# Turning K and P on VectorE instead of transposing them on TensorE, in a one-token attention layer

## The chip, the cores and the metric

The kernel runs on one core of a Trainium2 chip. The metric is the device time of one execution in microseconds (us); a smaller one is better. The four executions of the kernel before lie within 0.06% of each other (384.63 to 384.87 us). The profiles are of single executions, and the span of a profile is about 2 us shorter than the time. Engines are named as in the profile: PE is TensorE (PEld its weight loads), DVE is VectorE, ACT is ScalarE, POOL is GpSimd, and SP issues the DMA loads.

## The reference, cut to what matters

Four sequences each decode one token. The last 4096 positions of a cached K and V are attended to, with 16 K/V heads of 128 and two query heads for each; then come an output projection and a gated feed-forward layer. Nearly all of the bytes are K and V.

```python
B, Hq, Hkv, Dh, W = 4, 32, 16, 128, 4096
q = (layernorm(x) @ wq)                        # [B, Hq, Dh]
k = repeat(k_cache[:, :, Sk - W:, :], 2)       # bf16, 64 MiB of it are read
v = repeat(v_cache[:, :, Sk - W:, :], 2)       # 64 MiB
p = softmax(q @ k.T * Dh ** -0.5)
h = x + (p @ v) @ wo
out = h + ((relu(n(h) @ W_gate)) * (n(h) @ W_up)) @ W_down
```

## The kernel before

K and V come in 16 tiles of 4 MiB each (K0 to K15 and V0 to V15; a tile is one sequence and four K/V heads), through a ring of four slots in SBUF. A load into a slot waits until the last reader of the slot is done. A K tile has positions on its partitions, but this kernel's Q times K takes the 128 numbers of a head on the partitions, so TensorE transposes it, 128x128 at a time, into PSUM (2048 times, 140.3 us busy), and VectorE and ScalarE copy it out (87.0 and 123.0 us):

```python
def pe_tr(i):                       # 4 a tile; 32 transposes each
    for j in range(4):
        for u in range(8):
            ...
            pe(..., lambda e: e.transpose(out=bankb[TRB[j]][:, u * 128:(u + 1) * 128],
                                          in_=kn[:, t, :], identity=perm...))      # L425
def evac(i, j):
    dst = kT[i // 2 % 2][:, lo:lo + 1024]
    if j % 2 == 0: dve(..., e.tensor_copy(out=dst, in_=src), deps)                 # L439
    else:          act(..., e.copy(out=dst, in_=src), deps)                        # L441

def pe_qk(dd):                      # 2 a tile; 16 matmuls of 32 columns of weights each
    for a in range(4):
        for j in range(4):          # each j to 32 partitions of its own; 16 matmuls took 0.98 us
            pe(..., lambda e: e.matmul(bank[4 + w][32 * j:32 * j + 32, :],         # L457
                lhsT=qTm[:, b, 4 * qd + a, :], rhs=k[:, j, :, a, :], ...))

place((kind, g), off, TILE, ("TR", 4 * g + 3) if kind == "K" else ("PV", 4 * g + 3), ...)
#                           the last reader, which frees the slot
```

P is transposed on TensorE as well (128 times) and copied out under a mask by VectorE. Softmax, P times V, and the layers after attention are cut here.

Of the kernel before, what the change touches and what calls it, by code (L numbers as in the profile page):

```python
# [6 lines left out]
ALU = mybir.AluOpType  # L7
# [4 lines left out]
B = 4  # L12
# [9 lines left out]
NUNIT = 4 * NTILE  # L22
# [5 lines left out]
KTW = 8192  # L28
# [86 lines left out]
def bass_sequential_preLN__sliding_block_cached__glu_gated_reglu__decode_kernel(  # L115
# [12 lines left out]
    with ExitStack() as es:  # L128
# [12 lines left out]
        arena = sb("arena", [128, 2 * KTW + NSLOT * TILE], BF16)  # L141
# [6 lines left out]
        c_m4 = sb("c_m4", [128, 4, 32], FP32)  # L148
        c_qm = sb("c_qm", [128, 4, 32], FP32)
        c_e8 = sb("c_e8", [128, 8, 16], FP32)  # L150
        c_s4 = sb("c_s4", [128, 4, 4], FP32)
        perm = sb("perm", [128, 4, 32], BF16)
        m4 = sb("m4", [128, 4], FP32)
        par = sb("par", [128, 2], FP32)
        am8 = sb("am8", [128, 8], FP32)
# [16 lines left out]
        qTm = sb("qTm", [128, B, KVH, 32], BF16)  # L172
        stat = sb("stat", [128, B, 8], FP32)
        gm4 = sb("gm4", [1, 128], FP32)
        fq = sb("fq", [128, 4], FP32)
# [19 lines left out]

        kT = [arena[:, i * KTW:(i + 1) * KTW] for i in range(2)]
        slot0 = 2 * KTW

# [3 lines left out]
        TRB = (0, 1, 2, 3)  # L202
        s_ps = psb[:, 4:6, :].rearrange("p a b -> p (a b)")
        o_ps = bank[6]
        m_ps = bank[7]
        mb_ps = bankb[7]
# [25 lines left out]
        def add_kv(kind, g):  # L232
            b, qd = divmod(g, 4)
            s = ring_slot()
            off = slot0 + s * TILE
            cache = A_k_cache if kind == "K" else A_v_cache
            src = cache[b, 4 * qd:4 * qd + 4, SK - WIN:SK, :].rearrange("a (p t) d -> p a (t d)", p=32)
            place((kind, g), off, TILE, ("TR", 4 * g + 3) if kind == "K" else ("PV", 4 * g + 3),
                  lambda e: e.dma_start(out=arena[:, off:off + TILE], in_=src), key=f"slot{s}")
# [19 lines left out]
        for blk in range(2 * KTW // 64):  # L259
            owner[blk] = "QKEND"  # L260
# [24 lines left out]
        def kv(kind, i):  # L285
            off = land[(kind, i // 4)]
            return arena[:, off:off + TILE].rearrange("p (t d) -> p t d", d=DH)

# [5 lines left out]
        pool("c_perm0", lambda e: e.memset(perm[:, :, :], 0.0))  # L294
        pool("c_perm", lambda e: e.affine_select(out=perm[:, :, :], in_=perm[:, :, :], pattern=[[-1, 4], [-4, 32]],
                                                 compare_op=ALU.not_equal, fill=1.0, base=0, channel_multiplier=1), ["c_perm0"])
# [6 lines left out]
                                                compare_op=ALU.not_equal, fill=1.0, base=0, channel_multiplier=1), ["c_m40"])  # L303
        pool("c_ones", lambda e: e.memset(ones_f[:, :], 1.0))
# [20 lines left out]
        for j in range(4):  # L325
            pool(f"c_same{j + 1}", lambda e, j=j: e.affine_select(out=sameh[:, :, :], in_=sameh[:, :, :], pattern=[[0, 4], [-1, 32]],
                                                                compare_op=ALU.not_equal, fill=0.25, base=-32 * j,
                                                                channel_multiplier=1), [f"c_same{j}"])

        pool("c_toq0", lambda e: e.memset(toq[:, :, :, :], 0.0))  # L330
        for q in range(4):
# [10 lines left out]
        dve("c_am8", lambda e: e.tensor_copy(out=am8[:, :].rearrange("p (a h) -> p a h", h=2),  # L342
                                             in_=bass.AP(tensor=m4, offset=0, ap=[[4, 128], [1, 4], [0, 2]])), ["c_m4"])
        dve("c_qTm", lambda e: e.memset(qTm[:, :, :, :], 0.0))
# [23 lines left out]
        def pe_q():  # L368
# [4 lines left out]
            for c in range(DC):  # L373
                pe("TP1", lambda e, c=c: e.transpose(out=tpv[:, 32 + c * 4:32 + (c + 1) * 4],
                                                     in_=chunk(x_bf, xd_bf[:, :, :].rearrange("b r a -> b (r a)"), c),
                                                     identity=ident_b[0:B, 0:B]))
            for c in range(DC):
# [7 lines left out]
            for bk in range(2):  # L385
                for s in range(4):
                    blk = bk * 4 + s
                    pe(("QT", blk), lambda e, blk=blk: e.transpose(out=mb_ps[:, blk * 128:(blk + 1) * 128],
                                                                   in_=p_sb[:, blk * 128:(blk + 1) * 128], identity=ident_b[:, :]),
                       [f"qev{bk}"] if s == 0 else [])  # L390

        def dve_q():
# [5 lines left out]
            dve("xT", lambda e: e.tensor_copy(out=xT[:, :, :], in_=tpv[:, 32:52].rearrange("p (c b) -> p c b", b=B)))  # L398
            dve("qev0", lambda e: e.tensor_copy(out=p_sb[:, 0:512], in_=bank[4]), ["QMM"])
            for s in range(8):  # L400
                hh4, bk = s % 4, s // 4
                off = 34 * (bk * 8 + hh4 // 2) + hh4 % 2
                dst = bass.AP(tensor=qTm, offset=off, ap=[[B * KVH * 32, 128], [68, 4], [KVH * 32, B]])
                dve("qTm", lambda e, dst=dst, s=s: e.tensor_copy(  # L404
                    out=dst, in_=mb_ps[:, s * 128:(s + 1) * 128].rearrange("p (g b) -> p g b", b=32)[:, :, 0:4]),
                    [("QT", 7), "c_qTm"])
# [5 lines left out]
        def pe_tr(i):  # L412
            kn = kv("K", i)
            for j in range(4):
                for u in range(8):
                    t = j * 32 + i % 4 * 8 + u
                    deps = []
                    if u == 0:
                        deps = [("L", "K", i // 4)] if j == 0 else []
                        if i == 0:  # L420
                            deps.append("c_perm")
                        else:
                            deps.append(("EV", i - 1, j))
                    last = j == 3 and u == 7
                    o = pe(("TRJ", i, j), lambda e, j=j, u=u, t=t: e.transpose(  # L425
                        out=bankb[TRB[j]][:, u * 128:(u + 1) * 128], in_=kn[:, t, :],
                        identity=perm[:, :, :].rearrange("p a k -> p (a k)")), deps)
                    if last:
                        P.names[("TR", i)] = o

        def evac(i, j):
            lo = j * 2048 + i % 2 * 1024
            dst = kT[i // 2 % 2][:, lo:lo + 1024]
            src = bankb[TRB[j]][:, 0:1024]
            deps = [("TRJ", i, j)]
            if i >= 4:
                deps.append(("QK", i // 2 - 2))
            if j % 2 == 0:
                dve(("EV", i, j), lambda e: e.tensor_copy(out=dst, in_=src), deps)  # L439
            else:  # L440
                act(("EV", i, j), lambda e: e.copy(out=dst, in_=src), deps)  # L441

        def pe_qk(dd):
            g, w = divmod(dd, 2)
            b, qd = divmod(g, 4)
            k = kT[dd % 2].rearrange("p (j t a k) -> p j t a k", j=4, t=16, a=4)
            for a in range(4):
                for j in range(4):
                    deps = []
                    if a == 0:  # L450
                        deps.append(("EV", 2 * dd + 1, j))
                        if qd == 0 and j == 0:
                            if b == 0:
                                deps += ["qTm", "qev0", "qev1"]
                            else:
                                deps += [("EXP", b - 1, w), ("MAX", b - 1)]
                    o = pe(("QK", dd), lambda e, a=a, j=j: e.matmul(  # L457
                        bank[4 + w][32 * j:32 * j + 32, :], lhsT=qTm[:, b, 4 * qd + a, :], rhs=k[:, j, :, a, :],
                        start=(qd == 0 and a == 0), stop=(qd == 3 and a == 3), skip_group_check=True), deps)
            P.names["QKEND"] = o  # L460

        def softmax(b, w):
            if w == 0:
                dve(("MAX", b), lambda e: e.tensor_reduce(out=stat[:, b, 0:1], in_=s_ps, axis=AX.X, op=ALU.max, negate=True),  # L464
                    [("QK", 8 * b + 7)])
                dve(("NB", b), lambda e: e.tensor_scalar(out=stat[:, b, 1:2], in0=stat[:, b, 0:1], scalar1=SCALE, scalar2=None,  # L466
                                                         op0=ALU.mult), [("MAX", b)])
            act(("EXP", b, w), lambda e: e.activation(  # L468
                out=p_sb[:, 2048 * w:2048 * w + 2048].rearrange("p (k a) -> p k a", a=4),
                in_=bass.AP(tensor=psb, offset=(4 + w) * 512, ap=[[4096, 128], [1, 512], [0, 4]]), func=ACT.Exp,  # L470
                bias=stat[:, b, 1:2], scale=SCALE, accum_out=stat[:, b, 2 + 3 * w:3 + 3 * w]),
                [("NB", b), ("PT", b - 1, 3) if b else ("QT", 7)])

        def put_pT(b, r):
            for tl in range(8):
                deps = []
                if tl == 0:
                    deps = [("EXP", b, r // 2)]
# [246 lines left out]
```

## Time and profile before

| | before |
|---|---|
| time, median of 4 runs | 384.68 us |
| input queue's share of 16 engines' time | 97.4% |
| PE, DVE, ACT busy | 65%, 42%, 38% |

From the page of the kernel before: of its slices (40 equal parts of the span, each digit tenths of busy time; PEclk is the granted TensorE clock in tenths), its DMA queues (packets, MB, share of 16 engines) and its chain of waits (share of the span by line).

```profile
PE   0664999779492938893947667966759366026753
...
PEclk9997999999888796999796969996969657555597
DMA  8999999999999999999999999999999999999992
...
q1 hardware_dynamic: 6352, 159.59, 97.4%
...
DMA sb_arena<-in_A_k_cache_dram 53%; PE psb L425 18%; DMA sb_arena<-in_B_W_down_dram 8%; DMA sb_arena<-in_A_v_cache_dram 8%; PE psb L457 5%; PE psb L505 2%; PE psb L480 1%; DVE sb_pp L487 1%; ACT sb_pp L468 1%; SPq L280 0%; DVE sb_stat L464 0%; DVE sb_o_sel L516 0%; PE psb L539 0%; PE psb L530 0%; DVE sb_o_tmp L512 0%
```

DMA stands at 9 from the second slice to the last but one: the kernel is as fast as its loads. The chain passes through PE only where a transpose frees a slot; a load of K took 28.3 us (median) from issue to landing, where the queue, at 429 GB/s from 31 to 281 us, moves a tile in about 9.8 us (an estimate: 4.19 MB at that rate). So a load waits behind others for most of its time, and this wait should cost nothing (the repair v4 below, which has no transposes, takes the same time).

The groups of instructions that the change touches (line, engine, operation, shape, count, then busy us, mean ns of one, and the idle time before with what ended it):

```profile
L425 PE MATMUL psb<-sb_perm,sb_arena 128*128 128x128 bf16 x2048 | 140.3, 235 | 74.0 <-DMA sb_arena<-in_A_k_cache_dram 73.8
L441 ACT COPY sb_arena<-psb 128x1024 bf16<-128x1024 bf16 x128 | 123.0, 1021 | 141.1 <-PE psb L425 141.1
...
L439 DVE COPY sb_arena<-psb 128x1024 bf16<-128x1024 bf16 x128 | 87.0, 689 | 112.1 <-PE psb L425 111.6
...
L457 PE MATMUL psb<-sb_arena,sb_qTm 128*32 128x512 bf16 x512 | 38.0, 423 | 0.9 <-DVE sb_qTm L404 0.9
```

A mean of a matmul is its latency; matmuls overlap: the 512 of L457, at a mean of 423 ns, would add up to 217 us, and their busy time is 38.0 us. What one costs in a stream is the busy time over the count: the four-abreast QK matmuls of L457 cost 38.0 us / 512 = 74 ns each.

The prediction rests on two more lines, weight loads of 128 columns at full clock (granted clock 1.00 from 27.5 to 28.4 and from 370.8 to 371.6 us), from the view of one source line (duration ns min/median/max). L667 reads its weights at a step of 18 bytes, L388 contiguously.

```profile
L667 PEld LDWEIGHTS psb<-sb_ident_b,sb_pp x9: 138/145/159, 370.8 to 371.3; 128*128 128x128 bf16 x9
...
L388 PEld LDWEIGHTS psb<-sb_ident_b,sb_pp x8: 95/98/98, 27.6 to 28.0; 128*128 128x128 bf16 x8
```

### The profile page before, as it was taken

How to read it: one execution, taken by the hardware profiler on the slowest of the kernel's cores; microseconds unless marked ns; L12 is line 12 of the kernel's file. 1: busy time of each engine (PE TensorE's matmuls, PEld its weight loads, DVE VectorE, ACT ScalarE, POOL GpSimd, SP SyncE). 2: the span in 40 equal slices, each digit the busy share in tenths (PEclk: the TensorE clock that was granted, in tenths of full speed). 3: DMA queues.
4: the chain of work that ended last, by engine and by line, in shares of the span. 5: the costliest groups of instructions: out<-in, count | busy, mean ns of one | idle time of the engine just before them, and what ended most of it. 6: DMA issues, size and time to landing. Idle time of an engine off the chain costs nothing.

```text
span 382.6 us, 8170 instructions
## 1 busy us (share of the span) xinstructions
PE 248.7 (65%) x3781; PEld 185.9 (49%) x3781; DVE 159.0 (42%) x277; ACT 146.4 (38%) x162; POOL 8.7 (2%) x36
## 2 busy tenths in 40 slices
PE   0664999779492938893947667966759366026753
PEld 0643788557371726672726455745546222003532
DVE  3342565665342434774432426752516454002220
ACT  3341688836161524762433428542525401000010
POOL 7100000000000000000000000000000000000000
PEclk9997999999888796999796969996969657555597
DMA  8999999999999999999999999999999999999992
GB/s 329 439 433 432 410 421 437 434 433 433 425 423 433 427 433 435 427 420 433 437 430 435 424 428 427 427 428 439 437 432 415 421 436 451 416 431 426 416 411 113
DMA packets 6408, 160.09 MB, mean 418 GB/s; under 512 B 740, under 2 KB 744, under 8 KB 1384
## 3 DMA queue, kind: packets, MB, share of 16 engines
q1 hardware_dynamic: 6352, 159.59, 97.4%
q8 instruction: 29, 0.48, 0.5%
q14 instruction: 3, 0.02, 0.0%
q10 hardware_dynamic: 24, 0.01, 0.0%
HBM read 159.58 MB, written 0.00 MB: 417 GB/s over the span
## 4 chain that ended last, share of the span: by engine, by line
DMA 69%; PE 27%; DVE 2%; SPq 1%; ACT 1%; issue 0%
DMA sb_arena<-in_A_k_cache_dram 53%; PE psb L425 18%; DMA sb_arena<-in_B_W_down_dram 8%; DMA sb_arena<-in_A_v_cache_dram 8%; PE psb L457 5%; PE psb L505 2%; PE psb L480 1%; DVE sb_pp L487 1%; ACT sb_pp L468 1%; SPq L280 0%; DVE sb_stat L464 0%; DVE sb_o_sel L516 0%; PE psb L539 0%; PE psb L530 0%; DVE sb_o_tmp L512 0%
## 5 line engine op out<-in xcount | busy, mean ns | idle before, releaser
L425 PE MATMUL psb<-sb_perm,sb_arena 128*128 128x128 bf16 x2048 | 140.3, 235 | 74.0 <-DMA sb_arena<-in_A_k_cache_dram 73.8
L441 ACT COPY sb_arena<-psb 128x1024 bf16<-128x1024 bf16 x128 | 123.0, 1021 | 141.1 <-PE psb L425 141.1
L425 PEld LDWEIGHTS psb<-sb_perm,sb_arena 128*128 128x128 bf16 x2048 | 131.5, 106 | 89.3 <-DMA sb_arena<-in_A_k_cache_dram 79.8
L439 DVE COPY sb_arena<-psb 128x1024 bf16<-128x1024 bf16 x128 | 87.0, 689 | 112.1 <-PE psb L425 111.6
L505 PE MATMUL psb<-sb_arena,sb_pp 128*32 128x512 bf16 x512 | 35.9, 425 | 19.9 <-DMA sb_arena<-in_A_v_cache_dram 19.9
L457 PE MATMUL psb<-sb_arena,sb_qTm 128*32 128x512 bf16 x512 | 38.0, 423 | 0.9 <-DVE sb_qTm L404 0.9
L505 PEld LDWEIGHTS psb<-sb_arena,sb_pp 128*32 128x32 bf16 x512 | 12.9, 104 | 36.3 <-DMA sb_arena<-in_A_v_cache_dram 20.9
L512 DVE TENSOR_TENSOR sb_o_tmp<-psb,sb_qm 128x512 f32<-128x512 f32 x16 | 11.1, 692 | 41.2 <-PE psb L505 41.2
L487 DVE TENSOR_TENSOR sb_pp<-psb,sb_am 128x1024 bf16<-128x1024 bf16 x16 | 19.6, 1223 | 16.2 <-PE psb L480 16.2
L480 PE MATMUL psb<-sb_ident_b,sb_pp 128*128 128x128 bf16 x128 | 11.5, 242 | 15.8 <-DVE sb_pp L487 8.3
L468 ACT ACTIVATE sb_pp<-psb,sb_stat 128x2048 bf16<-128x2048 f32 x8 | 15.8, 1975 | 9.7 <-DVE sb_stat L466 9.7
L457 PEld LDWEIGHTS psb<-sb_arena,sb_qTm 128*32 128x32 bf16 x512 | 11.6, 103 | 14.8 <-issue 6.2
L480 PEld LDWEIGHTS psb<-sb_ident_b,sb_pp 128*128 128x128 bf16 x128 | 8.6, 108 | 18.8 <-ACT sb_pp L468 8.1
L516 DVE TENSOR_REDUCE sb_o_sel<-sb_o_tmp 128x128 f32<-128x512 f32 x16 | 16.4, 1024 | 0.5
L612 ACT COPY sb_pp<-psb 128x288 f32<-128x288 f32 x1 | 0.4, 399 | 36.2 <-PE psb L607 36.2
L654 PE MATMUL psb<-sb_arena,sb_hnT 128*32 128x384 bf16 x120 | 7.5, 421 | 4.1 <-DVE sb_hnT L639 2.2
L654 PEld LDWEIGHTS psb<-sb_arena,sb_hnT 128*32 128x32 bf16 x120 | 4.1, 121 | 7.2 <-DMA sb_arena<-in_B_W_up_dram 2.3
L464 DVE TENSOR_REDUCE sb_stat<-psb 128x1 f32<-128x1024 f32 x4 | 4.9, 1221 | 4.6 <-PE psb L457 4.6
L687 PE MATMUL psb<-sb_arena,sb_pp 128*32 128x144 bf16 x144 | 3.7, 251 | 4.1 <-DMA sb_arena<-in_B_W_down_dram 3.6
L534 ACT ACTIVATE sb_stat<-sb_stat 128x1 f32<-128x1 f32 x4 | 0.9, 213 | 13.1 <-DVE sb_stat L532 13.1
L661 DVE TENSOR_TENSOR sb_pp<-psb,sb_pp 128x384 bf16<-128x384 f32 x3 | 1.5, 551 | 9.6 <-PE psb L654 9.6
L687 PEld LDWEIGHTS psb<-sb_arena,sb_pp 128*32 128x32 bf16 x144 | 2.6, 105 | 5.1 <-DMA sb_arena<-in_B_W_down_dram 4.6
(128 smaller groups left out, 78.7 us busy)
## 6 DMA issues: line engine op xcount, KB each, us to landing
sb_arena<-in_A_k_cache_dram SPq DMA_DIRECT2D x16, 4096.0 KB, 28.3
sb_arena<-in_A_v_cache_dram SPq DMA_DIRECT2D x16, 4096.0 KB, 33.6
sb_arena<-in_A_wo_dram SPq DMA_DIRECT2D x1, 4608.0 KB, 20.7
sb_arena<-in_B_W_gate_dram SPq DMA_DIRECT2D x1, 4608.0 KB, 34.1
sb_arena<-in_B_W_up_dram SPq DMA_DIRECT2D x1, 4608.0 KB, 43.5
sb_arena<-in_A_wq_dram SPq DMA_DIRECT2D x1, 4096.0 KB, 23.0
sb_arena<-in_B_W_down_dram SPq DMA_DIRECT2D x3, 1296.0 KB, 30.0
sb_arena<-in_B_W_down_dram SPq DMA_DIRECT2D x1, 864.0 KB, 31.6
```

Source lines behind the costliest of these rows:

```text
L425: o = pe(("TRJ", i, j), lambda e, j=j, u=u, t=t: e.transpose(out=bankb[TRB[j]][:, u * 128:(u + 1) * 128], in_=kn[:, t, :], identity=perm[: ...
L439: dve(("EV", i, j), lambda e: e.tensor_copy(out=dst, in_=src), deps)
L441: act(("EV", i, j), lambda e: e.copy(out=dst, in_=src), deps)
L457: o = pe(("QK", dd), lambda e, a=a, j=j: e.matmul(bank[4 + w][32 * j:32 * j + 32, :], lhsT=qTm[:, b, 4 * qd + a, :], rhs=k[:, j, :, a, :], ...
L468: act(("EXP", b, w), lambda e: e.activation(out=p_sb[:, 2048 * w:2048 * w + 2048].rearrange("p (k a) -> p k a", a=4), in_=bass.AP(tensor=p ...
L480: pe(("PT", b, r), lambda e, tl=tl: e.transpose(out=mb_ps[:, tl * 128:(tl + 1) * 128], in_=p_sb[:, (r * 8 + tl) * 128:(r * 8 + tl + 1) * 128],
L487: dve(("PM", b, r), lambda e: e.tensor_tensor(out=dst, in0=src, in1=msk, op=ALU.mult), [("PT", b, r), "c_am8", ("PV", 16 * b - 1) if b els ...
L505: pe(("PV", i), lambda e, j=j, lo=lo, pm=pm, tb=tb: e.matmul(o_ps[32 * j:32 * j + 32, :], lhsT=pT[:, pm:pm + 32], rhs=v[:, lo:lo + 512], s ...
L512: dve(("OS", g), lambda e: e.tensor_tensor(out=o_tmp[:, :].rearrange("p (t d) -> p t d", t=4), in0=o_ps.rearrange("p (t d) -> p t d", t=4) ...
L516: dve(("OSEL", g), lambda e: e.tensor_reduce(out=o_sel[:, qd, :], in_=o_tmp[:, :].rearrange("p (t d) -> p d t", t=4), axis=AX.X, op=ALU.ad ...
L654: pe(("GU", g, c // 4), lambda e, g=g, m=m, j=j, lo=lo, c=c: e.matmul(bank[3 * g + m][32 * j:32 * j + 32, 0:384], lhsT=hnT[:, c if c < 4 e ...
L687: pe("DOWN", lambda e, j=j, r=r, n=n, wv=wv: e.matmul(bank[0][32 * n:32 * n + 32, 0:144], lhsT=hhT[:, r * 128 + 32 * j:r * 128 + 32 * j + 32],
```

## The change

Its intent is to take the transposes and their copies out of PE, PSUM and ACT. The change is written for a transpose on VectorE of 32x32 blocks of 4-byte elements, so that a pair of bf16 numbers moves as one element. K is turned so in place. In the layout meant, a partition then holds one pair index of 32, in each quarter of 32 partitions for other positions; a column holds a row of the tile, and the two numbers of a pair lie side by side. Q times K then needs q in blocks on the diagonal of a full 128x128 weight, one matmul for each head `a` and each of four parts `cb` of the 128 numbers. As the rows of a K tile are ordered position by position with the four heads inside (partition = 4 p + a), the columns of one head are every fourth pair: the moving operand steps by 8 elements, 16 bytes.

```diff
-            place((kind, g), off, TILE, ("TR", 4 * g + 3) if kind == "K" else ("PV", 4 * g + 3),
+            place((kind, g), off, TILE, ("QK", g, 1) if kind == "K" else ("PV", g),
...
-        def pe_tr(i): ...            # 32 transposes, 4 times a tile
-        def evac(i, j): ...          # and their copies out of PSUM
+        def turn_k(g, w):
+            k = arena[:, land[("K", g)] + w * QWW:][:, 0:QWW].bitcast(FP32)
+            dve(("TRA", g, w), lambda e: e.transpose(out=k, in_=k), ...)              # L420
...
         def pe_qk(g, w):
             for a in range(4):
-                for j in range(4):
-                        bank[4 + w][32 * j:32 * j + 32, :], lhsT=qTm[:, b, 4 * qd + a, :], rhs=k[:, j, :, a, :],
+                for cb in range(4):
+                    off = land[("K", g)] + w * QWW + cb // 2 * 64 + 2 * a + cb % 2
+                        bank[SB[b % 2] + w], lhsT=arena[:, wo_:wo_ + 128],            # L437
+                        rhs=bass.AP(tensor=arena, offset=off, ap=[[AW, 128], [128, 64], [8, 8]]),
...
+            for w in range(2):       # softmax: the scores read four times, masked by the bias, each time into another fourth of P
+                for a in range(4):
+                    act(("EXP", b, w), lambda e, w=w, a=a: e.activation(                # L458
+                        out=bass.AP(tensor=pp, offset=4096 + 2048 * w + a, ap=[[8192, 128], [4, 512]]), ...
+        def turn_p(b, w):            # instead of 128 TensorE transposes and masked copies
+            dve(("PTR", b, w), lambda e: e.transpose(out=dst, in_=src), ...)
```

Cut here: the code that lays q into the blocks, a second pair of PSUM banks for the scores, the softmax weights, and renamed waits. The work after attention is the same.

## The prediction

> **What bounds the kernel now.** The DMA queue. The view of DMA queues gives 160.09 MB and 97.4% of the time of all 16 engines for the input queue; the slices show DMA at 9 everywhere but at the ends, at 410 to 450 GB/s. PE is 65%, DVE 42%, ACT 38% busy. The chain of waits names K loads for 53% and the line of TensorE transposes for 18%, but that is how slots are released; about three loads are queued (28.3 us from issue to landing, for tiles of about 9.75 us), so the queue does not run dry.
>
> **What the change removes.** 2048 transposes (140.3 us of PE), their evacuations (ACT 123.0 us, DVE 87.0 us), 128 transposes of P (11.5 us) and their masked copies (19.6 us of DVE). Almost none of it delays the input queue, so the gain is about 0.
>
> **What it adds.**
> 1. 32 in-place turns of 128x4096 fp32 on DVE. [...] The trace's DVE operations of 512 and 1024 elements (692 and 1221 ns) give 1.03 ns per element, so an estimate of 4.4 us each, 8.8 us per K tile, 140 us in all. It fits beside 9.75 us (K alone) and 19.5 us (K and V).
> 2. QK: still 512 matmuls of 512 columns, but of full width, no longer four side by side. Before, 16 took 0.98 us, so four side by side 0.245 us. At that rate a K tile takes 7 to 8 us. But the moving operand now steps by 16 bytes. [...] The trace has a hint: weight loads of 128 columns with a step of 18 bytes took 145 ns, contiguous ones 98 ns, both at full clock. So I expect near 430 ns per matmul: 13.8 us per K tile, 220 us in all, above the 9.75 us at which the first K tiles arrive.
> 3. K0's slot is released only after q exists (about 31 us) and QK of K0 is done, no longer by transposes at 22 us.
>
> **On the critical path.** I played both cases through with these durations, four slots, queues in order. At 216 to 260 ns the queue runs dry once, before K3, for 1.5 to 3 us. At 430 ns: before K3 about 8 us, before V1 2.5 us, before K6 about 12 us (K4, softmax and PV come together), then hardly again, since K and V together give 19.5 us for 16 to 17 us of PE; 20 to 26 us in all. The tail (last weights, last matmuls) stays.
>
> **Prediction.** 402 us; 384.5 to 413 holds it 8 times in 10. Two humps: about 387 if the strided read is free, about 406 if it halves. Faster by over 2%: 0.03; within 2%: 0.40; slower by over 2%: 0.57.
>
> **What would show it.** QK matmuls spaced near 430 ns or near 216; DVE turns at 4.4 us; holes in the DMA slices at about 45 to 50 and 100 to 115 us and hardly any later; PE busy all through the first 120 us; ACT far down.
>
> **What would make it wrong.** Strided reads at full rate (then "same"); turns at twice my cost (then DVE binds too, 410 and more); QK above 450 ns, where PE binds later too and each 40 ns adds some 20 us; slots freed sooner than I think.

The 4.4 us of a turn follow from the 1.03 ns per element of the trace. The 430 ns of a QK matmul, and with them the 20 to 26 us of holes and the case of 406 us, stays as the author's estimate: twice the 216 ns (median) at which groups of four matmuls of the kernel before follow each other at full clock (L457 and L505). That such a read takes twice the time, no trace had shown; the weight loads alone say 145 / 98 = 1.48 times. The forecast came to 402 us, between the cases of 387 and 406.

## The result, and the profile after

The changed kernel takes 625.8 us (median of 4 runs, 624.17 to 626.28) against 384.68 us: the ratio is 1.626 (95% interval 1.6237 to 1.6283), 63% slower. Ratios here and below are the mean time of one kernel's fast runs over that of the other's of the same rounds, so not quite the ratio of the medians. The time lies far outside the predicted range.

The page of the changed kernel, the same parts as before:

```profile
PE   0399999995989999979989999969899999833556
...
PEclk9955555555565656555565656565655555566577
DMA  8971952606066484848092848483482929349996
...
q1 hardware_dynamic: 6352, 159.59, 60.6%
...
PE psb L437 71%; PE psb L480 6%; DMA sb_arena<-in_B_W_down_dram 5%; DMA sb_arena<-in_A_v_cache_dram 4%; DMA sb_arena<-in_A_wq_dram 3%; DVE sb_arena L420 2%; ACT sb_pp L458 2%; DVE sb_o_sel L492 1%; DVE sb_stat L444 1%; PE psb L382 1%; DVE sb_o_tmp L488 1%; PE psb L446 0%; PE psb L452 0%; DVE sb_pp L467 0%; ACT sb_arena L412 0%
```

PE and DMA have changed places. DMA has holes through the whole of the attention, not in the first 120 us alone, and PE is at 9 nearly everywhere, at half clock. 71% of the chain is the QK matmul. Its group and those of the other new work:

```profile
L437 PE MATMUL psb<-sb_arena 128*128 128x512 bf16 x512 | 441.5, 1035 | 6.7 <-DVE sb_arena L420 4.6
L420 DVE STREAM_TRANSPOSE sb_arena<-sb_arena 128x4096 f32<-128x4096 f32 x32 | 141.4, 4431 | 33.4 <-DMA sb_arena<-in_A_k_cache_dram 33.4
...
L458 ACT ACTIVATE sb_pp<-psb,sb_stat 128x512 bf16<-128x512 f32 x32 | 39.4, 1459 | 479.3 <-DVE sb_stat L453 479.3
```

QK costs 441.5 / 512 = 862 ns a matmul, twice what I had put down, and 27.6 us a K tile, where a K and a V tile together arrive in about 19.5 us (an estimate: 8.39 MB at the 429 GB/s of the kernel before). The turns cost 4.43 us each, as estimated. The waits of the DMA queue's own issuer (us in total, times, longest) say what held the loads:

```profile
SPq L240 <- PE psb L437: 482.8, 16, 55.1
```

That sum alone is no loss: in the contiguous kernel below the same wait adds up to 252.6 us while the queue is busy for 97.8%. The holes in the DMA slices are the loss.

Three readings of this trace narrow the cause before any experiment. First, the clock. Half clock could be the cause or the consequence. At the end of each of the first 12 PVs, give or take 0.7 us, the granted clock goes from 0.50 to 1.00 for 3.4 us (one ends at 214.30 us, and the clock is 1.00 from 214.87 to 218.29 us). From the timeline, here are the weight loads of four successive QK matmuls in such a stretch (start us, us):

```profile
215.07 0.12 PEld L437 LDWEIGHTS psb<-sb_arena 128*128 128x128 bf16 x1 [0.72 <-issue]
215.93 0.11 PEld L437 LDWEIGHTS psb<-sb_arena 128*128 128x128 bf16 x1 [0.74 <-issue]
216.78 0.12 PEld L437 LDWEIGHTS psb<-sb_arena 128*128 128x128 bf16 x1 [0.74 <-issue]
217.65 0.11 PEld L437 LDWEIGHTS psb<-sb_arena 128*128 128x128 bf16 x1 [0.74 <-issue]
```

And the view of that stretch (its length; busy us and count of PE, PEld, DVE, ACT, POOL; granted clock; DMA share; GB/s):

```profile
214.90:218.20 3.30, 3.30 (x5) 0.46 (x4) 3.27 (x3) 0.00 (x0) 0.00 (x0) 1.00 1.11 477
```

At a clock of 1.00 the matmuls are still 0.86 us apart. Over the whole trace the 19 gaps that lie in full clock have a median of 857 ns, and so have the 469 in half clock. So the clock is not the cause: the columns follow at 857 / 512 = 1.67 ns each at a clock of 1.00 as at 0.50. That the clock follows the access pattern is shown by a run below: with that pattern alone changed, the mean granted clock of the profiled run is 0.778 instead of 0.573.

Second, the company. VectorE turns K in place while QK runs. From 31.14 us on, QK ran without a pause for over 90 us. VectorE turned three tiles meanwhile, for 8.8 us each, and was idle for up to 61 us in between. Up to 141 us, the 24 spacings of QK that lie inside a turn have a median of 857 ns, the other 103 one of 859. So the turns do not slow it.

Third, the stages. From 31 to 141 us PE was busy for 109.86 of 110 us, all of it QK of the first four K tiles; no load can be called late there. The view of that stretch, with the columns as above:

```profile
31.00:141.00 110.00, 109.86 (x128) 15.76 (x128) 26.31 (x6) 1.30 (x5) 0.00 (x0) 0.50 0.47 196
```

What is left are the step of the moving operand, and the width of the matmul.

### The profile page after: what moved, and what is told of

The parts are those of the page before. It is cut to its first block, busy times and chain, and to the rows that moved or that the text cites. A ratio compares the mean times of both kernels' runs of the same rounds, so it can differ in the third digit from the quotient of the medians.

```text
span 623.9 us, 3670 instructions
## 1 busy us (share of the span) xinstructions
PE 531.7 (85%) x1629; PEld 102.0 (16%) x1629; DVE 209.7 (34%) x158; ACT 51.2 (8%) x94; POOL 16.2 (3%) x38
## 4 chain that ended last, share of the span: by engine, by line
PE 79%; DMA 12%; DVE 6%; ACT 2%; issue 0%; SPq 0%
PE psb L437 71%; PE psb L480 6%; DMA sb_arena<-in_B_W_down_dram 5%; DMA sb_arena<-in_A_v_cache_dram 4%; DMA sb_arena<-in_A_wq_dram 3%; DVE sb_arena L420 2%; ACT sb_pp L458 2%; DVE sb_o_sel L492 1%; DVE sb_stat L444 1%; PE psb L382 1%; DVE sb_o_tmp L488 1%; PE psb L446 0%; PE psb L452 0%; DVE sb_pp L467 0%; ACT sb_arena L412 0%
## 5 line engine op out<-in xcount | busy, mean ns | idle before, releaser
L437 PE MATMUL psb<-sb_arena 128*128 128x512 bf16 x512 | 441.5, 1035 | 6.7 <-DVE sb_arena L420 4.6
L420 DVE STREAM_TRANSPOSE sb_arena<-sb_arena 128x4096 f32<-128x4096 f32 x32 | 141.4, 4431 | 33.4 <-DMA sb_arena<-in_A_k_cache_dram 33.4
L437 PEld LDWEIGHTS psb<-sb_arena 128*128 128x128 bf16 x512 | 61.9, 123 | 368.4 <-issue 361.4
L458 ACT ACTIVATE sb_pp<-psb,sb_stat 128x512 bf16<-128x512 f32 x32 | 39.4, 1459 | 479.3 <-DVE sb_stat L453 479.3
L480 PE MATMUL psb<-sb_arena,sb_pp 128*32 128x512 bf16 x512 | 54.6, 605 | 21.8 <-DMA sb_arena<-in_A_v_cache_dram 14.9
L467 DVE STREAM_TRANSPOSE sb_pp<-sb_pp 128x2048 bf16<-128x2048 bf16 x8 | 18.0, 2281 | 1.9 <-ACT sb_pp L458 1.9
L382 PE MATMUL psb<-sb_arena,sb_xnT 128*32 128x512 bf16 x32 | 3.6, 631 | 8.8 <-DMA sb_arena<-in_A_wq_dram 8.8
L458 ACT ACTIVATION_READ_ACCUMULATOR sb_pp<-psb,sb_stat 128x1 f32 x32 | 10.2, 318 | 0.0
L298 POOL MEMSET sb_arena<- 128x8192 f32 x1 | 6.9, 6924 | 0.0
L412 ACT COPY sb_arena<-sb_q_keep 32x128 bf16<-32x128 bf16 x16 | 4.9, 305 | 2.0 <-DVE sb_q_keep L404 1.9
```

The costliest lines, as they stand in the source:

```text
L298: pool("c_qW", lambda e: e.memset(arena[:, 0:2 * QWW].bitcast(FP32), 0.0))
L382: pe("QMM", lambda e, c=c, w=w, g=g, bk=bk: e.matmul(bank[4 + bk][32 * g:32 * g + 32, :], lhsT=xnT[:, c + bk if c == 4 else c, :], rhs=w, ...
L412: act(("QW", b), lambda e, i=i: e.copy(out=bass.AP(tensor=arena, offset=32 * i * AW + b % 2 * QWW + 32 * i, ap=[[AW, 32], [128, 4], [514, ...
L420: dve(("TRA", g, w), lambda e: e.transpose(out=k, in_=k), [("L", "K", g)] if w == 0 else [])
L437: pe(("QK", g, w), lambda e, off=off, wo_=wo_, qd=qd, first=first, last=a == cb == 3: e.matmul(bank[SB[b % 2] + w], lhsT=arena[:, wo_:wo_ ...
L458: act(("EXP", b, w), lambda e, w=w, a=a: e.activation(out=bass.AP(tensor=pp, offset=4096 + 2048 * w + a, ap=[[8192, 128], [4, 512]]), in_= ...
```

## The experiments

The kernels marked wrong read other elements of K than they should. They keep every instruction, wait and shape of the changed kernel. The comparison with the reference passed them too, since the scores of these inputs are small and the softmax nearly flat; so it does not vouch for an order of K. For the repairs (v1 to v5) I worked the order out element by element on indices against the changed kernel's.

### Four steps of the moving operand in one kernel (wrong)

A line, in this and the later texts, is a stretch of 16 bytes within a partition. That the price goes by lines is a theory, called LINE, for the runs to test.

```diff
-   rhs=bass.AP(tensor=arena, offset=off, ap=[[AW, 128], [128, 64], [8, 8]])
+   batch 0: [[AW, 128], [128, 64], [8, 8]]     batch 1: [[AW, 128], [128, 64], [4, 8]]
+   batch 2: [[AW, 128], [128, 64], [2, 8]]     batch 3: [[AW, 128], [128, 64], [1, 8]]
+   (off without the term 2 * a + cb % 2 + cb // 2 * 64)
```

> The changed kernel with the QK moving operand read at another step in each of the four batches (wrong results on purpose; the same 16 x 32 matmuls, the same widths, weights and waits): 8 runs of 8 elements as now at step 8 (16 bytes) in batch 0, step 4 (8 bytes) in batch 1, step 2 in batch 2, step 1 in batch 3. Theory LINE: each time the next column lies in another 16-byte line the moving operand costs about 1.67 ns (857 ns over 512 columns), at whatever clock; more columns of the same line come free up to the array's rate. Then the four groups are spaced about 857, 430, 216 and 216 ns (430 where the granted clock is 0.5), and the whole is about 455 to 465 us. Rival STEP: any step over 1 costs the full price: 857, 857, 857, 216 and about 560 us. Rival WIDE: it is the full-width 128x128 matmul with new weights each time, or the turns in place running beside it, not the step: 857 in all four and 626 us.

One run, 455.31 us. Each batch has a source line of its own; L441, L443, L445, L447 are batches 0 to 3:

```profile
L441 PE MATMUL psb<-sb_arena 128*128 128x512 bf16 x128 | 110.2, 1037 | 2.1 <-ACT sb_arena L412 2.1
L443 PE MATMUL psb<-sb_arena 128*128 128x512 bf16 x128 | 55.8, 607 | 6.0 <-DVE sb_arena L420 6.0
...
L447 PE MATMUL psb<-sb_arena 128*128 128x512 bf16 x128 | 38.0, 469 | 13.1 <-DVE sb_arena L420 13.1
...
L445 PE MATMUL psb<-sb_arena 128*128 128x512 bf16 x128 | 35.8, 442 | 14.2 <-DVE sb_arena L420 14.1
```

Busy time over 128 gives 861, 436, 280 and 297 ns. The last two mix full and half clock; their gaps in full clock have medians of 217 and 216 ns. So WIDE falls: full-width matmuls with new weights run at 216 ns. STEP falls too: a step of 4 bytes costs nothing (217 against 216 ns), and one of 8 bytes half as much as one of 16 (436 and 861 ns), as the lines that they touch say. LINE stands. (This trace has no clock record before 155.4 us, so the full clock that its page shows for batch 0 is not measured.)

### Patterns that part the line from the step (wrong)

```diff
+   batch 0: [[AW, 128], [128, 64], [7, 8]]           batch 1: [[AW, 128], [128, 64], [16, 8]]
+   batch 2: [[AW, 128], [128, 64], [16, 4], [1, 2]]  batch 3: [[AW, 128], [128, 64], [1, 4], [8, 2]]
```

> As d1_steps, with patterns that part lines from steps (wrong results on purpose). Batch 0: step 7 (14 bytes; 8 columns touch 7 lines): LINE says 7/8 of 857, about 750 ns. Batch 1: step 16 (32 bytes): LINE says 857 as at 16 bytes; if the step itself mattered, about twice that. Batch 2: two adjacent columns, then 32 bytes on: LINE says half, 430 ns, although the average step is 16 bytes; a price on the step of the outer dimension would say 857. Batch 3: the same two lines visited in turn, one column from each (step 8 inside, step 1 outside, so only 2 distinct lines in 8 columns): 857 if what counts is that the next column lies in another line, about 216 if lines just read are kept. Whole about 540 to 565 us under LINE.

One run, 527.86 us. L441 to L447 are again batches 0 to 3:

```profile
L443 PE MATMUL psb<-sb_arena 128*128 128x512 bf16 x128 | 118.1, 1096 | 4.6 <-DVE sb_arena L420 4.6
L441 PE MATMUL psb<-sb_arena 128*128 128x512 bf16 x128 | 109.4, 1036 | 2.1 <-ACT sb_arena L412 2.1
...
L447 PE MATMUL psb<-sb_arena 128*128 128x512 bf16 x128 | 69.2, 699 | 0.0
L445 PE MATMUL psb<-sb_arena 128*128 128x512 bf16 x128 | 56.1, 610 | 1.4 <-DVE sb_arena L420 1.4
```

Two of four came as LINE said. Two neighbours and then a jump of 32 bytes cost 56.1 / 128 = 438 ns, half, although the average step is 16 bytes. A step of 32 bytes costs 923 ns, 7% over 16 bytes and not twice. The others were misses: step 7 cost 855 ns where its 7 lines out of 8 columns should give 750, and two lines visited in turn cost 541 ns, neither 857 nor 216. The whole is also under the 540 to 565 us expected.

### More patterns, to see whether lines or pairs of columns count (wrong)

```diff
+   batch 0: [[AW, 128], [128, 64], [3, 8]]   batch 1: [[AW, 128], [128, 64], [5, 8]]
+   batch 2: [[AW, 128], [128, 64], [6, 8]]   batch 3: [[AW, 128], [128, 64], [1, 4], [4, 2]]
```

> More patterns for the moving operand, wrong results on purpose. Steps 3, 5 and 6 (6, 10 and 12 bytes; 8 columns touch 3, 5 and 6 lines) in batches 0 to 2, and in batch 3 a walk within single lines (0, 8, 2, 10, 4, 12, 6, 14 bytes). LINE as first stated, 1.67 ns per line touched: 321, 536, 643 ns and 216. The other reading, after 853 ns for step 7: columns are fetched in fixed pairs of neighbours, and only a pair in one line is cheap: step 3 has pairs (0,6) (12,18) (24,30) (36,42) bytes, two of four split; step 5 and 6 nearly all split, so near 640 for step 3 and 750 to 857 for steps 5 and 6, and 216 to 430 for the walk within lines.

One run, 432.86 us. The medians of the gaps are 347 ns (step 3, full clock), 573 (step 5) and 687 (step 6, both clocks alike), and 216 ns for the walk within lines at full clock. LINE had said 321, 536, 643 and 216, and is low by 7 to 8%; pairs had said 640 and 750 to 857, and fall. Put together, the price of a line is 1.67 to 1.68 ns (steps of 8 and 16 bytes) or 1.79 to 1.81 ns (6, 10, 12, 32 bytes): 687 ns / (512 x 6/8 lines) = 1.79. Step 7 and the alternation are the two patterns that this does not give; why, stays open.

### QK contiguous, nothing else (wrong)

```diff
-   ap=[[AW, 128], [128, 64], [8, 8]]
+   ap=[[AW, 128], [1, 512]]
```

> The changed kernel with nothing but the QK moving operand made contiguous, 512 columns in a row (wrong results on purpose). LINE, and the view that all of the slowdown comes through QK: QK spaced 216 ns at full clock and 427 at half, the input queue nearly full again apart from one hole of 1 to 4 us before K3, 386 to 390 us, so within 2% of before. If the rest of the change (turns in place, more EXP instructions, K0's slot freed later) had a cost of its own, the time stays clearly over 390 us.

Measured: 382.66 us, ratio to before 0.9935 (0.9919 to 0.9952). Of this kernel's page:

```profile
DMA  8999999999999999999999999999999999999993
...
q1 hardware_dynamic: 6352, 159.59, 97.8%
...
L437 PE MATMUL psb<-sb_arena 128*128 128x512 bf16 x512 | 140.4, 439 | 54.7 <-DVE sb_arena L420 52.7
```

So one access pattern is the whole of the slowdown, all 243 us. The rest of the change, with its turns, its 32 EXP instructions and K0's slot freed later, costs nothing that shows. The hole of 1 to 4 us before K3 that the expectation allowed for does not show in the slices either, and the time is under its 386 to 390 us. It is even 2 us faster than the kernel before. The page has 3670 instructions here and 8170 before, and 0.20 MB of instruction loads against 0.48 MB in the same 16 engines; that could be a part of it, but no run parted it.

### A repair on VectorE's side (right results)

```diff
-   e.transpose(out=k, in_=k)
+   e.transpose(out=k.rearrange("p (n a l) -> p n l a", a=4, l=8), in_=k.rearrange("p (n l a) -> p n l a", a=4, l=8))
...
-   off = ... + 2 * a + cb % 2          [[AW, 128], [128, 64], [8, 8]]
+   off = ... + 16 * a + cb % 2         [[AW, 128], [128, 64], [2, 8]]
```

> A repair with right results: the turn of K writes each block of 32 columns in another order (the 8 keys of one head side by side), so QK reads at step 2 (4 bytes), 4 columns to a line. LINE: QK spaced about 216 ns at full clock. If VectorE writes 4-byte elements at 32-byte steps at its old rate, the turns stay at 4.43 us and the time is 386 to 390 us as for c1_contig. If VectorE pays per line as well, the turns go to 6 to 8 us and the time to about 394 (6 us) or 440 us (8 us), with VectorE as the new bound.

Measured: 413.08 us, ratio 1.075 (1.0707 to 1.0792). QK is at 216 ns at full clock, but from the page:

```profile
L420 DVE STREAM_TRANSPOSE sb_arena<-sb_arena 128x4096 f32<-128x4096 f32 x32 | 235.9, 7419 | 4.8 <-DMA sb_arena<-in_A_k_cache_dram 4.8
```

With its writes scattered, 4 bytes at a time, a turn took 7.42 us on VectorE against 4.43. The price moved to VectorE, which now bounds the stage where K tiles come alone: from 30 to 140 us it was busy for 99.9 us, at a DMA share of 0.83 (0.96 from 140 to 300 us). The edit also makes the access pattern of the turn one of more dimensions; no run had that without the scattered writes. This is the second case of the expectation, and the time lies between the two that stand there for 6 and 8 us.

### A repair by the order of the rows in the load (right results)

To bring the rows into the order "quarter, head, position", the load of a K tile was written as four loads of 32 partitions.

```diff
-   cache[...].rearrange("a (p t) d -> p a (t d)", p=32)                     # one load of 128 partitions
+   rows = cache[...].rearrange("a (i l t) d -> i a l (t d)", i=4, l=8)       # for K: four loads
+   dma_start(out=arena[32 * i:32 * i + 32, off:off + TILE], in_=rows[i])     # i = 0..3
    (QK reads as in the repair before)
```

> The repair without VectorE's price, with right results: K's rows are laid into the partitions in another order by the load (four loads of 32 partitions, 1 MB each, for a K tile[...]), so that the 8 keys of one head are neighbours in each block of 32. The turn writes in its plain order, QK reads at step 2. Theory (only the moving operand's step cost the time): QK spaced 216 ns at full clock, turns 4.43 us as in the changed kernel, input queue full, 381 to 384 us as c1_contig (382.66), that is about 0.5% below the kernel before. Rival: loads of 32 partitions use the 16 DMA engines less well; then the DMA slices sink below those of c1_contig and the time goes over 390 us.

Measured: 996.65 us, ratio 2.5911 (2.5867 to 2.5955). The time is the rival's, and by far. The view of the stretch from 40 to 100 us (columns as above; the last two are DMA share and GB/s):

```profile
40.00:100.00 60.00, 14.73 (x104) 5.85 (x104) 10.96 (x11) 3.02 (x9) 0.00 (x0) 0.81 0.25 108
```

A quarter of the DMA engines' time was used, 108 GB/s, where the contiguous kernel's same stretch had a share of 1.00 and 428 GB/s. About four of these loads were issued and not yet done at a time, and they still did not add up. The records of DMA packets say more: in this stretch 4 packets were under way at nearly every moment, in the contiguous kernel 16, and a packet of 32 KB took the same 1213 ns in both. So the packets were not slower; by the share of 0.25, three quarters of the engines' time had none. Why is not shown. The edit changed two things at once: each load goes to 32 partitions instead of 128, and the outermost dimension of its source is now the 4 heads, where it was 32 blocks of positions. Four packets at a time would fit the 4 heads, but no run parted the two.

### The same with wq loaded first (right results)

```diff
-   add_kv("K", 0); <load wq>; <load wq, last rows>
+   <load wq>; <load wq, last rows>; add_kv("K", 0)
...
-   turn_k(0, 0); turn_k(0, 1); pe_q(); act_q(); dve_q(); ...
+   pe_q(); act_q(); dve_q(); ...; turn_k(0, 0); turn_k(0, 1)
```

> v2_rows with the load of wq ahead of K0's, and the first turn after q's work in VectorE's order (right results). It tests the third point of the prediction, that K0's slot is freed late because QK waits for q: K3's load then goes into wq's slot, free at about 17 us, and the queue holds two loads more at 40 us. If there is a hole before K3, it goes and the time falls by 1 to 3 us against v2_rows of the same rounds; if the queue had no hole there, the two are the same within 0.3%.

Measured: 983.16 us, 13.5 us below the run before, which is neither of the two cases expected (1 to 3 us, or the same). The loads were the bound (a DMA share of 0.25 from 31 to 100 us in both), so it says nothing of the hole that it was made for, and where the 13.5 us come from stays open. It is repeated below on a good base.

### Strided weights (wrong)

```diff
-   lhsT=arena[:, wo_:wo_ + 128], rhs=<step 8>
+   lhsT=bass.AP(tensor=arena, offset=b % 2 * QWW, ap=[[AW, 128], [s, 128]]), rhs=arena[:, off:off + 512]
+   s = 1, 8, 9, 16 in batches 0, 1, 2, 3
```

> Contiguous moving operand, but weights of 128 columns at step 1, 8, 9 and 16 (2, 16, 18 and 32 bytes) in batches 0 to 3, wrong results on purpose. It tests the hint of the prediction: that the price of weight loads at a step of 18 bytes (145 against 98 ns) tells the price of the moving operand. If both pay 1.67 ns per column in a line of its own, the weight loads go to 215 ns or more at steps 8, 9, 16. If they stay near 145 ns (0.4 ns per column more), weights are read another way and the hint could not have told the price.

One run, 381.38 us. The view of the four source lines, in the order of s (duration ns min/median/max):

```profile
L440 PEld LDWEIGHTS psb<-sb_arena x128: 95/98/151, 31.2 to 66.6; 128*128 128x128 bf16 x128
L442 PEld LDWEIGHTS psb<-sb_arena x128: 141/145/308, 74.5 to 136.7; 128*128 128x128 bf16 x128
L444 PEld LDWEIGHTS psb<-sb_arena x128: 137/138/304, 148.9 to 214.1; 128*128 128x128 bf16 x128
L446 PEld LDWEIGHTS psb<-sb_arena x128: 140/147/309, 226.6 to 292.1; 128*128 128x128 bf16 x128
```

Weights at 16, 18 and 32 bytes take 138 to 147 ns, 98 contiguously: 0.3 to 0.4 ns more per column, not the (857 - 216) / 512 = 1.25 of the moving operand. The number that I took for a hint was right, but it belongs to another operand, and the moving operand paid over three times as much.

### A repair by loading each head in 8 KB runs (right results)

```diff
-   cache[...].rearrange("a (p t) d -> p a (t d)", p=32)       # runs of 32 KB
+   cache[...].rearrange("a (p t) d -> p a (t d)", p=128)      # K only: runs of 8 KB, one load of 128 partitions
...
-   [[AW, 128], [128, 64], [8, 8]]
+   [[AW, 128], [128, 16], [2, 32]]                           # 32 positions of one head side by side
...
-   EXP in_=bank[SB[b % 2] + w]
+   EXP in_=bass.AP(tensor=psb, offset=SB[b % 2] * 512 + 2 * w, ap=[[4096, 128], [1, 2], [32, 32], [4, 8]])
```

> A repair with right results that asks neither VectorE nor narrow loads for it: K is loaded with 128 runs of 8 KB for each head (whole tile still one load over all 128 partitions), so every column of a turned block belongs to one head, QK reads 32 neighbours at step 2 (4 columns to a line), and EXP puts the scores back in the old order by its read of PSUM. Theory (the moving operand's lines were the whole slowdown): QK spaced 216 ns at full clock, turns 4.43 us, DMA at 9 in all slices, 382 to 386 us[...]. If packets of 8 KB are much slower than those of 32 KB, or EXP from a strided PSUM read gets much longer, over 390 us.

Measured: 384.88 us, ratio to before 1.0005 (0.9992 to 1.0019): the same, with right results. Of its page:

```profile
q1 hardware_dynamic: 12496, 159.59, 98.5%
...
L423 DVE STREAM_TRANSPOSE sb_arena<-sb_arena 128x4096 f32<-128x4096 f32 x32 | 141.6, 4436 | 67.9 <-DMA sb_arena<-in_A_k_cache_dram 67.9
L440 PE MATMUL psb<-sb_arena 128*128 128x512 bf16 x512 | 144.1, 446 | 53.7 <-DVE sb_arena L423 51.6
```

It is 2.2 us over the contiguous kernel. Its input queue was busy for 98.5% against 97.8% for the same bytes, and in the records of DMA packets an 8 KB packet has a median of 313 ns, where a quarter of a 32 KB one's 1216 is 304. That fits the loss; no run had the one without the other.

### wq first, on that base (right results)

The edit is that of the other run with wq first.

> v4_head with wq loaded ahead of K0 and the first turn after q's work (right results): the test of the prediction's third point that v3_wqfirst could not give, since there the loads were the bound. If the late release of K0's slot leaves a hole before K3's load, it goes here and the time falls by 0.5 to 3 us against v4_head of the same rounds; if the queue is never empty there, both are the same within 0.2%.

Measured: 384.82 us against 384.88 in the same rounds, the same within 0.02%. With QK at 216 ns the queue had no hole before K3 that was worth anything. The 1.5 to 3 us of the prediction for this case are not there.

### EXP writing neighbours (wrong)

EXP is the exponential of the softmax, on ScalarE; this is the contiguous kernel with one more edit.

```diff
-   out=bass.AP(tensor=pp, offset=4096 + 2048 * w + a, ap=[[8192, 128], [4, 512]])
+   out=pp[:, 4096 + 2048 * w + 512 * a:4096 + 2048 * w + 512 * (a + 1)]
```

> c1_contig with the EXP instructions writing 512 neighbours instead of every fourth element of P (wrong results on purpose). EXP took 1459 ns for 512 columns in the changed kernel, where ScalarE's other 512-column copy took 586 ns. If ScalarE pays for writes at a step of 8 bytes, EXP falls to 600 to 700 ns; if it is the bias, the accumulator or the read of PSUM, it stays near 1430. The whole stays within 0.3% of c1_contig's 382.66 us, as EXP is not what the input queue waits for.

Measured: 381.95 us, ratio to before 0.993, within 0.2% of the contiguous kernel. EXP's line of this kernel (1459 ns in the changed kernel):

```profile
L458 ACT ACTIVATE sb_pp<-psb,sb_stat 128x512 bf16<-128x512 f32 x32 | 21.5, 697 | 245.1 <-DVE sb_stat L453 245.1
```

So on ScalarE too the scattered writes took about double: 1426 ns in the contiguous kernel, at steps of 8 bytes, against 697 for 512 neighbours. But it is off the path.

### QK at just the price that was predicted (wrong)

```diff
-   off = ... + 2 * a + cb % 2        [[AW, 128], [128, 64], [8, 8]]
+   off = ... + cb % 2                [[AW, 128], [128, 64], [4, 8]]
```

> The changed kernel with the QK moving operand at step 4 (8 bytes, two columns to a line) in all batches, wrong results on purpose: QK then costs just what the prediction assumed, about 430 ns (431 in d1_steps). It tests whether only that one figure of the prediction was wrong. If the playing through of queues, slots and stages was right, the time is 403 to 411 us, with the input queue dry before K3 and K6 and hardly later. If the time is under 395 or over 420 us, the prediction was wrong in the schedule too.

Measured: 400.72 us, ratio to before 1.0417 (1.04 to 1.0435). Of its page:

```profile
DMA  8999699977199999999999999999999999999994
GB/s 343 421 441 426 267 421 448 448 316 318 53 421 420 421 419 454 434 425 421 426 448 438 425 420 434 438 439 425 421 433 431 448 425 360 409 431 421 464 398 204
...
L437 PE MATMUL psb<-sb_arena 128*128 128x512 bf16 x512 | 222.6, 607 | 15.4 <-DVE sb_arena L420 13.3
```

A slice is 9.95 us. The holes are in slice 5 (40 to 50 us) and in slices 9 to 11 (80 to 109 us), and hardly any come later. That is where the prediction put them for 430 ns. The time is 2 us under the range of the expectation and 5 us under the 406 of the prediction's case of half rate, so the schedule was played through a little too darkly, but no more than that.

## Why the prediction was wrong, point by point

- **"What bounds the kernel now. The DMA queue", and a gain of about 0.** Right. With QK repaired, all of the removed work (140.3 us of PE, 210 us of copies) is worth nothing: 384.88 against 384.73 us of the kernel before in the same rounds.
- **"an estimate of 4.4 us each" for the turns.** Right: 4.43 us, 4431 ns / 4096 = 1.08 ns per element against the 1.03 of VectorE's plain operations in the prediction.
- **"So I expect near 430 ns per matmul: 13.8 us per K tile".** This is the step that failed. That the step would cost time was right, and its size was off by two: 862 ns, 27.6 us per K tile, 441.5 us in all. The difference, 512 x (862 - 430) ns = 221 us, added to the 406 us of the case of half rate, gives 627 us; 625.8 was measured. PE bounds the whole of the attention then, so nearly every microsecond of it counts, as the last paragraph of the prediction had said of "QK above 450 ns".
- **Why 430?** It had two sources. One was the weight loads, 145 against 98 ns. The runs with strided weights show the same 145 ns (138 to 147) for 16 bytes and over, and a moving operand at the same step pays 1.25 ns more per column instead of 0.4. The other no trace had shown, so the halving was my estimate. By the runs a line of which two columns are read gives half of the full rate (436 ns a matmul), one column a quarter (861), and only four columns the full rate (217).
- **"K0's slot is released only after q exists".** True of the order, but worth nothing where QK runs at 216 ns: 384.82 against 384.88 us. In the changed kernel the first gap, from about 45 us on, comes from QK at 862 ns; K3's load was issued at 58.8 us.
- **"16 to 17 us of PE" against 19.5 us for K and V together, so hardly a hole later.** It follows from the wrong figure. At step 4, where the figure is true, the holes are where the prediction put them and the time is 400.72 us. So the rest of the schedule, taken together, was off by some 5 us.
- **The range.** I had two cases in mind, full rate and half rate, and set the upper end of the range by the second. The hint measured another operand, so the range had to hold worse rates too. The same profile held a warning: VectorE's reduce of 512 elements at large steps (L516) took 1024 ns, where its product of 512 contiguous ones (L512) took 692; these are two operations, so it was a warning and no proof.

## What to carry to other kernels

Before a layout is changed to save work on one engine, look at how each operand that streams will step through memory, and measure a stream of just that instruction: here a step of 16 bytes instead of 2 cost the fourfold time of every QK matmul and 243 us of the whole. A price taken from one operand (weights, at most 0.4 ns more per column) did not carry over to another (the moving operand, 1.25). And when the loads are the bound, taking work off the other engines gained nothing here (384.88 against 384.73 us). There was only time to lose, and each repair should be asked where its own scattered access goes, as the write on VectorE and the reordered load showed.

## What the runs showed, in one place

- **TensorE's moving operand:** two bf16 columns per line of 16 bytes ran at half of the full rate (436 ns for 512 columns), one at a quarter (861), four at the full one (217 at full clock): about 1.67 to 1.81 ns per line, as long as that is more than the contiguous read took (216 ns at full clock, 427 at half). At a step of 16 bytes and at one of 12 it was the same at either granted clock (857 and 687 ns). Step 7 (855) and two lines in turn (541) do not fit.
- **The largest step that was free** at full clock was 2 bf16 (217 ns), with 3 at 347 ns; a step of 8 cost four times the contiguous read (861 against 217).
- **The granted clock:** in the changed kernel PE was busy 109.86 of 110 us (31 to 141 us), and the granted clock was 0.50 for that stretch. In the runs the clock went with the rate at which the matmuls followed each other: the spacings that lie in full clock are 412 of 499 at 431 ns (step 4 in all batches), 110 of 124 at 535 ns (two lines in turn), 22 of 124 at 573 ns (step 5) and 19 of 499 at 857 ns (the changed kernel). So a PE that was busy, but slowly fed, was held at half clock here.
- **Strided weights:** the loads took 138 to 147 ns at 16 to 32 bytes against 98, far less than the moving operand paid.
- **ScalarE's writes at 8-byte steps:** 1426 ns in the contiguous kernel against 697 for 512 neighbours.
